# Thirty-two bytes behind the operands: where the rows and buffers that TensorE reads begin in an attention and feed-forward kernel

## The chip, the cores and the metric

The kernel runs on one core of one Trainium2 chip, in one launch. The metric is the time of one execution on the device, in microseconds. Three runs of the kernel before took 712.76, 710.11 and 710.58 us; the median is 710.58 us. One further execution was recorded by the hardware profiler; all rows of the profile come from it.

## The reference

Two attentions in a row, then a feed-forward layer, all in float32. There are 8 batches of 8 heads with 576 tokens and 64 values a head, and 32 learned pack queries a head.

```python
def sm_attn(qq, kk, vv):
    s = scale * np.matmul(qq, kk.transpose(0, 1, 3, 2))
    s = s - np.max(s, axis=-1, keepdims=True)
    a = np.exp(s)
    a = a / (np.sum(a, axis=-1, keepdims=True) + 1e-09)
    return np.matmul(a, vv)
p_packed = sm_attn(p, k, v)                   # 32 packs per head
out = sm_attn(q, p_packed, p_packed)          # each token attends to the packs
...
x = out.transpose(0, 2, 1, 3).reshape(8 * 576, 512)
h = x @ w_in                                  # 512 -> 2048
g = h * (1.0 / (1.0 + np.exp(-h)))
return g @ w_out                              # 2048 -> 512
```

## The kernel before

**Staging.** Per batch, the first attention turns k, v and the pack queries into 32 packed rows a head, and the second gives each token its 32 shares of these rows (a softmax). The product of shares and packed rows isn't formed by itself: the packed rows are first multiplied by w_in (`Packs`, line 461 is the end of it), which gives a matrix from the 256 shares of a token to the 2048 hidden values, and the shares are multiplied by that. So the hidden layer is `h_products` (lines 479 to 489), and the second layer is `products` and `out_products` (lines 516 to 543).

**Halves.** The large products take operands in the type float32r, each number split into an upper part, rounded to that type, and a lower part, the difference. A product is three matmuls: upper by upper, upper by lower, lower by upper. That holds for w_out (`wo_hi`, `wo_lo`, written once, lines 200 and 204), for the shares (`a2_hi`, `a2_lo`, written in `upper2` and `lower2`), for the packs times w_in (`pw_hi`, `pw_lo`, lines 458 and 461) and for the hidden values (`g_hi`, `g_lo`, lines 508 and 514). ScalarE writes the upper parts, VectorE the lower ones.

**Units.** The hidden layer is cut into 16 rows f of 128 values. A unit is one batch and one f: `h_products` makes 12 matmuls of 128x288 columns (two halves of the 576 tokens, two shares of heads, three parts), with a slice of a pack buffer as the stationary operand and a share buffer as the moving one. `h_values` then makes the sigmoid-weighted g of 512 tokens; the 64 tokens left are kept in `rest`, and two batches' rest is done together in four further units. `out_products` makes 12 matmuls of 128x512 columns, with 128 columns of `g_hi` or `g_lo` stationary and a row f of `wo_hi` or `wo_lo` moving. It runs two units behind `h_products`. There are 1536 matmuls of line 489 and 1728 of line 521 in the program.

**Order.** The order of the engines' instructions is written by hand: a list of steps (`ORDER`) for the first two batches, in which w_in and w_out are also decoded from 64-bit loads and split, and the loop over `units` at the end for the other six, in which one step of the next batch's attention is put between units. TensorE, VectorE, ScalarE and SyncE run in that order.

**Buffers.** A pool gives out its buffers in turn. The pack and g pools have two buffers a name, and after the first two batches a third is added in the space that the staging of the weights left (`pw_b`, `gp_b`), so three are in use. The shares have four a name: two halves of the tokens for each of two batches. `wo_hi` and `wo_lo` are one tile each, 16 rows of 512 numbers. Buffers lie one behind the other in the order of the pools.

Of the kernel before, what the change touches and what calls it, by code (L numbers as in the profile page):

```python
# [9 lines left out]
F32 = mybir.dt.float32  # L10
F32R = mybir.dt.float32r
# [4 lines left out]
ALU = mybir.AluOpType  # L16
# [3 lines left out]
P = 128  # L20
# [3 lines left out]
HS = S // 2  # L24
NB = HS // 32
DM = H * D
DFF = 2048
NF = DFF // P
NJ = 4
JW = DFF // NJ  # L30
# [52 lines left out]
def packed_attention_ffn(ctx: ExitStack, tc: tile.TileContext, pkT, qT, vA, vB, w_in, w_out, out):  # L83
# [13 lines left out]
    nc = tc.nc  # L97
    ent = ctx.enter_context
    const = ent(tc.tile_pool(name="const", bufs=1))
    kvq = ent(tc.tile_pool(name="kvq", bufs=2))  # L100
    pw = ent(tc.tile_pool(name="pw", bufs=2))
    a2p = ent(tc.tile_pool(name="a2p", bufs=4))
# [7 lines left out]
    ident = const.tile([P, P], F32, name="ident")  # L110
    make_identity(nc, ident)
    win = const.tile([P, NF, NI, P], I32, name="win")
    wo_hi = const.tile([P, NF, DM], F32R, name="wo_hi")
    wo_lo = const.tile([P, NF, DM], F32R, name="wo_lo")

    rest = const.tile([P, NF, 2, 2, REST], F32, name="rest")
    parts = tc.dram_tile((EARLY, 2, P, 2, DM), F32, name="parts")
# [1 line left out]
    made = {}  # L119
# [34 lines left out]
    class Weights:  # L154
# [38 lines left out]

        def both(self, n):
            f, nf, _ = CHUNKS[n]
            return (t[:, f : f + nf].rearrange("p i n -> p (i n)") for t in (wo_hi, wo_lo))

        def upper(self, n):
            hi, _ = self.both(n)
            nc.scalar.copy(hi, self.raw[n][1].bitcast(F32))  # L200

        def lower(self, n):
            hi, lo = self.both(n)
            nc.vector.tensor_tensor(lo, self.raw[n][1].bitcast(F32), hi.bitcast(F32), ALU.subtract)  # L204

    def heads(bank, lhs, rhs):

# [8 lines left out]
    class Attention:  # L216
# [205 lines left out]
            nc.vector.transpose(s2, e2)  # L422

        def upper2(self, hf):
            hi = a2p.tile([P, 2, HS], F32R, name="a2_hi")
            lo = a2p.tile([P, 2, HS], F32R, name="a2_lo")
            made["a2", self.b, hf] = hi, lo
            a2 = self.back[hf][:, :, :HS] if self.b in ON_TOKENS else self.half[hf][0].rearrange("p (r s) -> p r s", r=2)
            self.shares[hf] = a2
            nc.scalar.copy(hi, a2)  # L430
# [5 lines left out]
    class Packs:  # L436
# [13 lines left out]
        def upper(self):  # L450
            b, j = self.b, self.f // FJ
            if self.f % FJ == 0:
                n = NJ * (b - EARLY) + j
                pool = pw_b if n > 0 and n % 3 == 1 else pw
                made["pw", b, j] = [pool.tile([P, 2, JW], F32R, name=name) for name in ("pw_hi", "pw_lo")]
            c = slice(self.f % FJ * P, (self.f % FJ + self.nf) * P)
            self.hi, self.lo = (t[:, :, c] for t in made["pw", b, j])
            nc.scalar.copy(self.hi, self.ps[:, :, : self.nf * P])  # L458
# [32 lines left out]
    def h_values(u, hf=None):  # L491
        b, f, *more = units[u]
        if hf is None or hf == 0:
            pool = gp_b if u > n_early and (u - n_early) % 3 == 1 else gp
            g_hi = pool.tile([P, 512], F32R, name="g_hi")
            g_lo = pool.tile([P, 512], F32R, name="g_lo")
            if more:
                g = rest[:, f : f + FJ].rearrange("p f e h s -> p (f e h s)")
                nc.scalar.copy(g_hi, g)
                hidden[u] = g, g_hi, g_lo  # L500
                return
            hidden[u] = gp.tile([P, 512], F32, name="g", bufs=1), g_hi, g_lo
        g, g_hi = (x.rearrange("p (h s) -> p h s", h=2) for x in hidden[u][:2])
        ps, to = made.pop(("h", u, hf)), rest[:, f, b % 2]
        if hf is not None:
            ps, to, g, g_hi = ps[:, 0], to[:, hf], g[:, hf], g_hi[:, hf]
        nc.scalar.activation(g, ps[..., :MAIN], AF.Silu)  # L507
        nc.scalar.activation(g_hi, ps[..., :MAIN], AF.Silu)  # L508
        nc.scalar.activation(to, ps[..., MAIN:HS], AF.Silu)  # L509
# [64 lines left out]
    def load_parts(b):  # L574
# [21 lines left out]
        "wl": weights.lower,  # L596
        "h": h_products,
        "g": h_values,
        "l": h_lower,
        "o": out_products,  # L600
# [21 lines left out]
    def hidden_up_to(u):  # L622
        nonlocal done
        while done < min(u, len(units) - 1):
            done += 1
            if len(units[done]) == 2:
                h_products(done)
            h_values(done)
            h_lower(done)
# [116 lines left out]
```

## Time and profile before

| | us |
|---|---|
| median of three runs | 710.58 |
| lowest and highest run | 710.11, 712.76 |
| span of the profiled execution | 711.0 |
| TensorE busy (matmul) | 692.0 |
| VectorE busy | 336.7 |
| ScalarE busy | 326.7 |
| GpSimd busy | 18.0 |

The span is from the first to the last instruction of the profiled execution; no other time is listed for it, and it lies 0.4 us above the median of the runs. Busy times are the union of an engine's instructions. In a row of a group, the first number behind the bar is the union of the busy time of the group, the second the mean duration of one in ns; matmuls overlap, so that a duration is longer than the distance between two starts. Behind the second bar stands how long the engine was idle just before instructions of the group, and what ended that. The operands are named by the program's tiles, output before the arrow.

### The profile page before, as it was taken

How to read it: one execution, taken by the hardware profiler on the slowest of the kernel's cores; microseconds unless marked ns; L12 is line 12 of the kernel's file. 1: busy time of each engine (PE TensorE's matmuls, PEld its weight loads, DVE VectorE, ACT ScalarE, POOL GpSimd, SP SyncE). 2: the span in 40 equal slices, each digit the busy share in tenths (PEclk: the TensorE clock that was granted, in tenths of full speed). 3: DMA queues.
4: the chain of work that ended last, by engine and by line, in shares of the span. 5: the costliest groups of instructions: out<-in, count | busy, mean ns of one | idle time of the engine just before them, and what ended most of it. 6: DMA issues, size and time to landing. Idle time of an engine off the chain costs nothing.

```text
span 711.0 us, 12198 instructions
## 1 busy us (share of the span) xinstructions
PE 692.0 (97%) x5098; PEld 567.0 (80%) x5098; DVE 336.7 (47%) x506; ACT 326.7 (46%) x614; POOL 18.0 (3%) x16
## 2 busy tenths in 40 slices
PE   6789999999999999999999999999999999999997
PEld 4567787878878888888878888878878788888886
DVE  4899997665353336331552315533362333622112
ACT  4577887554434426362532625453352532533221
POOL 0011111110000000000000000000000000000000
PEclk9999999999999999999999999999999999999999
DMA  9858255705012130312111121021301210010002
GB/s 327 322 168 349 76 185 183 265 1 185 1 60 82 33 139 1 111 33 87 67 60 61 39 88 67 27 100 36 137 1 59 83 35 1 1 60 1 0 1 74
DMA packets 31509, 64.15 MB, mean 90 GB/s; under 512 B 19424, under 2 KB 19424, under 8 KB 27104
## 3 DMA queue, kind: packets, MB, share of 16 engines
q1 hardware_dynamic: 31360, 63.26, 25.5%
q8 instruction: 40, 0.66, 0.4%
q10 hardware_dynamic: 96, 0.13, 0.1%
q14 instruction: 13, 0.11, 0.0%
HBM read 47.71 MB, written 11.53 MB: 83 GB/s over the span
## 4 chain that ended last, share of the span: by engine, by line
PE 89%; DVE 6%; DMA 2%; issue 1%; ACT 1%; SPq 0%; DVEq 0%; ACTq 0%
PE ps_acc L521 54%; PE ps_two L489 27%; PE ps_two L211 6%; DMA kvq_t<-in_qT 2%; PE ps_two L309 1%; DVE g_lo L514 1%; DMA kvq_t<-in_pkT 1%; DVE wo_lo L204 1%; DVE win L185 1%; DVE win L191 1%; DVE win L184 0%; DVE win L192 0%; PE ps_acc L211 0%; DVE pw_lo L461 0%; DVE w_raw L184 0%
## 5 line engine op out<-in xcount | busy, mean ns | idle before, releaser
L521 PE MATMUL ps_acc<-wo_hi,g_hi 128*128 128x512 f32 x576 | 229.2, 398 | 0.0
L521 PE MATMUL ps_acc<-wo_lo,g_hi 128*128 128x512 f32 x576 | 225.4, 391 | 0.8 <-DVE wo_lo L204 0.8
L521 PE MATMUL ps_acc<-wo_hi,g_lo 128*128 128x512 f32 x576 | 225.3, 391 | 0.0
L514 DVE TENSOR_TENSOR g_lo<-g,g_hi 128x512 fp32r<-128x512 f32 (+1 forms) x132 | 90.8, 688 | 261.3 <-ACT g_hi L508 261.3
L507 ACT ACTIVATE g<-ps_two 128x512 f32<-128x512 f32 (+1 forms) x132 | 77.5, 587 | 271.2 <-PE ps_two L489 245.6
L489 PE MATMUL ps_two<-a_hi,pw_hi 128*128 128x288 f32 x512 | 152.3, 298 | 2.6 <-DVE pw_lo L461 1.7
L489 PE MATMUL ps_two<-a_lo,pw_hi 128*128 128x288 f32 x512 | 151.5, 296 | 0.0
L489 PE MATMUL ps_two<-a_hi,pw_lo 128*128 128x288 f32 x512 | 150.6, 294 | 0.0
L521 PEld LDWEIGHTS ps_acc<-wo_hi,g_hi 128*128 128x128 f32 x576 | 108.0, 188 | 40.2 <-issue 19.1
L521 PEld LDWEIGHTS ps_acc<-wo_hi,g_lo 128*128 128x128 f32 x576 | 108.1, 188 | 24.4 <-DVE g_lo L514 0.8
L521 PEld LDWEIGHTS ps_acc<-wo_lo,g_hi 128*128 128x128 f32 x576 | 108.2, 188 | 19.6 <-DVE wo_lo L204 1.5
L489 PEld LDWEIGHTS ps_two<-a_hi,pw_hi 128*128 128x128 f32 x512 | 96.4, 188 | 8.1 <-DVE pw_lo L461 2.0
L489 PEld LDWEIGHTS ps_two<-a_lo,pw_hi 128*128 128x128 f32 x512 | 96.1, 188 | 3.5
L489 PEld LDWEIGHTS ps_two<-a_hi,pw_lo 128*128 128x128 f32 x512 | 96.2, 188 | 0.0
L508 ACT ACTIVATE g_hi<-ps_two 128x512 fp32r<-128x512 f32 (+1 forms) x132 | 76.7, 581 | 7.3 <-PE ps_acc L521 7.3
L461 DVE TENSOR_TENSOR pw_lo<-ps_two,pw_hi 128x1024 fp32r<-128x1024 f32 (+1 forms) x35 | 38.3, 1126 | 15.0 <-ACT pw_hi L458 15.0
L458 ACT CAST pw_hi<-ps_two 128x1024 fp32r<-128x1024 f32 (+1 forms) x35 | 31.6, 943 | 21.9 <-PE ps_two L211 21.9
L211 PE MATMUL ps_two<-win,ppT 64*32 64x512 f32 (+1 forms) x560 | 32.5, 560 | 0.4 <-DVE ppT L332 0.4
L509 ACT ACTIVATE rest<-ps_two 128x64 f32<-128x64 f32 (+1 forms) x132 | 30.5, 231 | 0.0
L507 ACT ACT_TABLE_LOAD x15 | 19.2, 1283 | 0.7 <-DVE g_lo L514 0.6
L211 PEld LDWEIGHTS ps_two<-win,ppT 64*32 64x32 f32 x560 | 8.0, 105 | 14.2 <-issue 10.9
L179 ACT ACTIVATE w_raw<-w_raw 128x1024 int32<-128x1024 uint32 (+1 forms) x13 | 13.3, 1021 | 9.5 <-DMA w_raw<-in_w_in 6.2
(101 smaller groups left out, 445.5 us busy)
## 6 DMA issues: line engine op xcount, KB each, us to landing
kvq_t<-in_pkT SPq DMA_DIRECT2D x7, 1216.0 KB, 5.4
kvq_t<-in_vA SPq DMA_DIRECT2D x8, 1024.0 KB, 6.9
out<-o SPq DMA_DIRECT2D x16, 512.0 KB, 2.9
kvq_t<-in_qT SPq DMA_DIRECT2D x7, 1152.0 KB, 5.1
w_raw<-in_w_in SPq DMA_DIRECT2D x6, 1024.0 KB, 8.4
win<-in_w_out SPq DMA_DIRECT2D x3, 1024.0 KB, 6.5
w_raw<-in_w_out SPq DMA_DIRECT2D x3, 1024.0 KB, 4.9
tm<-tm SPq DMA_DIRECT2D x56, 40.0 KB, 2.0
```

Of the source, the lines that this page charges most:

```text
L179: nc.scalar.activation(low, low.bitcast(U32), AF.Copy, scale=2.0**-29)
L185: nc.vector.scalar_tensor_tensor(low, up, -(2**31), low, op0=ALU.bitwise_and, op1=ALU.bitwise_or)
L191: nc.vector.tensor_scalar(z, up, 3, None, op0=ALU.logical_shift_left)
L211: nc.tensor.matmul(bank(par)[NP * i : NP * i + NP], lhs(r, i), rhs(r, i), start=True, stop=True)
L458: nc.scalar.copy(self.hi, self.ps[:, :, : self.nf * P])
L461: nc.vector.tensor_tensor(self.lo, self.ps[:, :, : self.nf * P], self.hi.bitcast(F32), ALU.subtract)
L489: nc.tensor.matmul(bank, p[:, par, cols], a[:, par], start=(n == 0), stop=(n == len(todo) - 1))
L507: nc.scalar.activation(g, ps[..., :MAIN], AF.Silu)
L508: nc.scalar.activation(g_hi, ps[..., :MAIN], AF.Silu)
L509: nc.scalar.activation(to, ps[..., MAIN:HS], AF.Silu)
L514: nc.vector.tensor_tensor(g_lo[:, c], g[:, c], g_hi[:, c].bitcast(F32), ALU.subtract)
L521: nc.tensor.matmul(bank, g[:, rows], w[:, f], start=(first and n == 0), stop=(last and n == 2))
```

## The change

w_out's halves get rows of 520 numbers, of which 512 are used. Each buffer of the shares, of g's halves and of the packs gets 8 numbers more at its end, which nothing reads or writes. The copies that split w_out take their source and target as rows instead of one flat run, since the target is no longer one. The rest of the program, its order, the number of instructions and the numbers that are computed stay as they are. `both` (line 194 and on) gives the two halves' rows of a chunk of one or two.

```diff
@@ -110,8 +110,8 @@
     ident = const.tile([P, P], F32, name="ident")
     make_identity(nc, ident)
     win = const.tile([P, NF, NI, P], I32, name="win")
-    wo_hi = const.tile([P, NF, DM], F32R, name="wo_hi")
-    wo_lo = const.tile([P, NF, DM], F32R, name="wo_lo")
+    wo_hi = const.tile([P, NF, DM + 8], F32R, name="wo_hi")[:, :, :DM]
+    wo_lo = const.tile([P, NF, DM + 8], F32R, name="wo_lo")[:, :, :DM]
 
     rest = const.tile([P, NF, 2, 2, REST], F32, name="rest")
     parts = tc.dram_tile((EARLY, 2, P, 2, DM), F32, name="parts")
@@ -193,15 +193,15 @@
 
         def both(self, n):
             f, nf, _ = CHUNKS[n]
-            return (t[:, f : f + nf].rearrange("p i n -> p (i n)") for t in (wo_hi, wo_lo))
+            return (t[:, f : f + nf] for t in (wo_hi, wo_lo))
 
         def upper(self, n):
             hi, _ = self.both(n)
-            nc.scalar.copy(hi, self.raw[n][1].bitcast(F32))
+            nc.scalar.copy(hi, self.raw[n][1].bitcast(F32).rearrange("p (f n) -> p f n", n=DM))
 
         def lower(self, n):
             hi, lo = self.both(n)
-            nc.vector.tensor_tensor(lo, self.raw[n][1].bitcast(F32), hi.bitcast(F32), ALU.subtract)
+            nc.vector.tensor_tensor(lo, self.raw[n][1].bitcast(F32).rearrange("p (f n) -> p f n", n=DM), hi.bitcast(F32), ALU.subtract)
 
     def heads(bank, lhs, rhs):
 
@@ -422,8 +422,8 @@
             nc.vector.transpose(s2, e2)
 
         def upper2(self, hf):
-            hi = a2p.tile([P, 2, HS], F32R, name="a2_hi")
-            lo = a2p.tile([P, 2, HS], F32R, name="a2_lo")
+            hi = a2p.tile([P, 2 * HS + 8], F32R, name="a2_hi")[:, : 2 * HS].rearrange("p (r s) -> p r s", r=2)
+            lo = a2p.tile([P, 2 * HS + 8], F32R, name="a2_lo")[:, : 2 * HS].rearrange("p (r s) -> p r s", r=2)
             made["a2", self.b, hf] = hi, lo
             a2 = self.back[hf][:, :, :HS] if self.b in ON_TOKENS else self.half[hf][0].rearrange("p (r s) -> p r s", r=2)
             self.shares[hf] = a2
@@ -452,7 +452,10 @@
             if self.f % FJ == 0:
                 n = NJ * (b - EARLY) + j
                 pool = pw_b if n > 0 and n % 3 == 1 else pw
-                made["pw", b, j] = [pool.tile([P, 2, JW], F32R, name=name) for name in ("pw_hi", "pw_lo")]
+                made["pw", b, j] = [
+                    pool.tile([P, 2 * JW + 8], F32R, name=name)[:, : 2 * JW].rearrange("p (r s) -> p r s", r=2)
+                    for name in ("pw_hi", "pw_lo")
+                ]
             c = slice(self.f % FJ * P, (self.f % FJ + self.nf) * P)
             self.hi, self.lo = (t[:, :, c] for t in made["pw", b, j])
             nc.scalar.copy(self.hi, self.ps[:, :, : self.nf * P])
@@ -492,8 +495,8 @@
         b, f, *more = units[u]
         if hf is None or hf == 0:
             pool = gp_b if u > n_early and (u - n_early) % 3 == 1 else gp
-            g_hi = pool.tile([P, 512], F32R, name="g_hi")
-            g_lo = pool.tile([P, 512], F32R, name="g_lo")
+            g_hi = pool.tile([P, 512 + 8], F32R, name="g_hi")[:, :512]
+            g_lo = pool.tile([P, 512 + 8], F32R, name="g_lo")[:, :512]
             if more:
                 g = rest[:, f : f + FJ].rearrange("p f e h s -> p (f e h s)")
                 nc.scalar.copy(g_hi, g)
```

A number has four bytes, so a row of w_out's halves takes 2080 bytes in place of 2048, a share buffer 2336 in place of 2304, a g half 2080 in place of 2048, and a pack buffer 4128 in place of 4096.

## The prediction

> **What bounds the kernel now.** I read the page first (share of each engine, the chain that ended last, the costliest groups), then the chain in order of time, then the timeline of TensorE in a quiet stretch.
>
> ```profile
> PE 692.0 (97%) x5098; PEld 567.0 (80%) x5098; DVE 336.7 (47%) x506; ACT 326.7 (46%) x614; POOL 18.0 (3%) x16
> PE 89%; DVE 6%; DMA 2%; issue 1%; ACT 1%; SPq 0%; DVEq 0%; ACTq 0%
> L521 PE MATMUL ps_acc<-wo_hi,g_hi 128*128 128x512 f32 x576 | 229.2, 398 | 0.0
> L521 PE MATMUL ps_acc<-wo_lo,g_hi 128*128 128x512 f32 x576 | 225.4, 391 | 0.8 <-DVE wo_lo L204 0.8
> L521 PE MATMUL ps_acc<-wo_hi,g_lo 128*128 128x512 f32 x576 | 225.3, 391 | 0.0
> L489 PE MATMUL ps_two<-a_hi,pw_hi 128*128 128x288 f32 x512 | 152.3, 298 | 2.6 <-DVE pw_lo L461 1.7
> L489 PE MATMUL ps_two<-a_lo,pw_hi 128*128 128x288 f32 x512 | 151.5, 296 | 0.0
> L489 PE MATMUL ps_two<-a_hi,pw_lo 128*128 128x288 f32 x512 | 150.6, 294 | 0.0
> ```
>
> TensorE holds 89% of the chain, and before these two lines it was idle for 3.4 us in all. So the kernel ends when TensorE has got through its list: 3 x 576 = 1728 matmuls of 512 columns (line 521) and 3 x 512 = 1536 of 288 columns (line 489). Both operands of every one of these 3264 lie in the buffers that the change pads. The means of 391 to 398 and 294 to 298 ns aren't what one costs, since matmuls overlap: what counts is how far apart they start. That stands in the timeline (start, duration, engine, line, operands):
>
> ```profile
> 373.20 0.29 PE L489 MATMUL ps_two<-a_hi,pw_hi 128*128 128x288 f32 x1
> ...
> 374.67 0.29 PE L489 MATMUL ps_two<-a_hi,pw_lo 128*128 128x288 f32 x1
> ...
> 375.94 0.39 PE L521 MATMUL ps_acc<-wo_hi,g_lo 128*128 128x512 f32 x1
> ...
> 377.30 0.39 PE L521 MATMUL ps_acc<-wo_hi,g_lo 128*128 128x512 f32 x1
> 377.53 0.29 PE L489 MATMUL ps_two<-a_hi,pw_hi 128*128 128x288 f32 x1
> 377.66 0.29 PE L489 MATMUL ps_two<-a_lo,pw_hi 128*128 128x288 f32 x1
> 377.79 0.29 PE L489 MATMUL ps_two<-a_hi,pw_lo 128*128 128x288 f32 x1
> 377.92 0.30 PE L489 MATMUL ps_two<-a_hi,pw_hi 128*128 128x288 f32 x1
> 378.06 0.29 PE L489 MATMUL ps_two<-a_lo,pw_hi 128*128 128x288 f32 x1
> ...
> 378.99 0.29 PE L489 MATMUL ps_two<-a_hi,pw_lo 128*128 128x288 f32 x1
> ...
> 380.27 0.39 PE L521 MATMUL ps_acc<-wo_hi,g_lo 128*128 128x512 f32 x1
> ...
> 381.63 0.39 PE L521 MATMUL ps_acc<-wo_hi,g_lo 128*128 128x512 f32 x1
> ```
>
> Between 375.94 and 377.30 lie six starts of line 521: 1.36 / 6 = 226.7 ns each. The unit after it, with another g buffer and another row of w_out, has 1.36 / 6 again. Line 489 starts 12 matmuls from 373.20 to 374.67 and 12 from 377.53 to 378.99: (1.47 + 1.46) / 22 = 133.2 ns each. The two lines differ by 224 columns and 93.5 ns, 0.417 ns a column. So 512 columns stream in 213.7 ns and 288 in 120.2, and **some 13 ns of each matmul don't depend on its length**. Over all of them this fixed part is 3264 x 13 = 42.4 us, 6.0% of the span. If the places of the operands cost TensorE anything now, it sits in there: the rest is columns.
>
> **Where the operands begin now.** By the shapes, every tile up to the g buffers that these matmuls read is a multiple of 128 bytes long: w_out's halves 32768 bytes with rows of 2048, a share buffer 2304, a pack buffer 4096, a g buffer 2048. So whatever the buffer, row or slice, all operands begin at the same place within 128 bytes. Whether larger differences of place matter, the chain in order of time can tell (start, length, what):
>
> ```profile
> 223.84 3.19 PE ps_two L489 x24
> 227.03 2.77 PE ps_acc L521 x12
> 241.30 2.77 PE ps_acc L521 x12
> 362.41 10.95 PE ps_acc L521 x48
> 572.92 3.19 PE ps_two L489 x24
> 591.10 2.77 PE ps_acc L521 x12
> ```
>
> From 227 to 591 us the units go through 16 rows of w_out, three g buffers, three pairs of pack buffers and all share buffers, in ever new pairs, and the lengths of like pieces repeat to the hundredth of a microsecond: 2.77 for 12 of line 521, 3.19 for 24 of line 489. Steps of 128 bytes and more therefore change nothing. What the trace can't show is a step below 128 bytes, and that is just what the change brings.
>
> **The change part by part.**
>
> *w_out's halves.* A row grows from 2048 to 2080 bytes, so row f begins 32 f bytes further on: at 0, 32, 64 and 96 within 128 bytes in turn. Three of four moving streams of line 521 begin elsewhere than now. No matmul is added or gets longer. The direct cost at TensorE is nothing or unknown, bounded below.
>
> *Splitting w_out (lines 200 and 204).* The copies and subtractions now write rows with a gap. No instruction is added. A 1024-element one covers two rows, and the dearest reading is that it costs as much as two of one row:
>
> ```profile
> L200 ACT CAST wo_hi<-win x5: 674/1130/1178, 46.2 to 104.4; 128x1024 fp32r<-128x1024 f32 x3, 128x512 fp32r<-128x512 f32 x2
> L200 ACT CAST wo_hi<-w_raw x5: 653/1133/1153, 17.0 to 149.8; 128x1024 fp32r<-128x1024 f32 x3, 128x512 fp32r<-128x512 f32 x2
> L204 DVE TENSOR_TENSOR wo_lo<-w_raw,wo_hi x5: 679/1216/1225, 18.2 to 152.6; 128x1024 fp32r<-128x1024 f32 x3, 128x512 fp32r<-128x512 f32 x2
> ```
>
> The two-row forms from w_raw take 1133 and 1216 ns, twice the one-row form would be 1306 and 1358: at most 173 + 142 = 315 ns for each of six pairs (three that come from w_raw and three from win), 1.9 us if all of it were on the path. A gap between rows is no new instruction, and the idle rows show TensorE waiting 0.8 us for line 204 in all, so I take nothing and keep 1.9 us as the end. Below nothing I see no reason.
>
> *Shares, g and packs.* Successive buffers step by 32 bytes. Of four share buffers, two g_hi and two g_lo, two pw_hi and two pw_lo, each kind is spread over the places within 128 bytes; the slices inside one buffer stay 512 or 1152 bytes apart, so they keep its place. ScalarE and VectorE do the same work on them. Should that become dearer, it is covered:
>
> ```profile
> L514 DVE TENSOR_TENSOR g_lo<-g,g_hi 128x512 fp32r<-128x512 f32 (+1 forms) x132 | 90.8, 688 | 261.3 <-ACT g_hi L508 261.3
> L507 ACT ACTIVATE g<-ps_two 128x512 f32<-128x512 f32 (+1 forms) x132 | 77.5, 587 | 271.2 <-PE ps_two L489 245.6
> ```
>
> VectorE stands idle 261.3 us ahead of g_lo and ScalarE 271.2 us ahead of g, and no row above has TensorE waiting for g. If a tenth came on top of both (9.1 and 7.8 us), this cover would swallow it.
>
> *TensorE's streams, the one term that decides.* Cost from both sides. The gain can't exceed the fixed part, 42.4 us. A loss is sized by the same rows: 13 ns are some 31 columns at 0.417 ns, and 31 columns of four bytes are about 128 bytes. If a stream paid for each 128-byte piece that it touches, one that starts inside a piece would touch one more, and pay 13 ns. I take zero, because it is nearest to the row that there is (no difference over all larger steps), and keep both ends.
>
> The Trainium skill, "TensorE: Matmul & The Clock Gate" (Step-by-step: what each phase is for), speaks against a gain: weights and moving data have independent read ports, so that loading the next weights takes nothing from the running matmul; by it the term is zero. The same page (Back-to-back issue gap) gives N/2.4 + 2.5 ns between warm matmuls, 215.8 ns for 512 columns; the trace has 226.7, so there are some 10.9 ns that this rule doesn't explain, as an estimate 18.8 us over the 1728 matmuls of this kind. "SBUF — State Buffer" (Door 1: The DMA port swizzle) counts in lines of 16 bytes; padding of 32 bytes would then make no stream touch one line more, which speaks against the loss. No run here shows lines or ports as such.
>
> *Sum.* 711.0 us of span, plus 0 for the streams, plus 0 for the rest: 711.0 us. The median of the runs shown is 710.58, the profiled span 0.4 us above it, so the time forecast is **710.6 us**. Within 0.5% (3.6 us, about what a measurement of this kernel can tell from no change) counts as the same.
>
> **The rivals.**
>
> *Faster: the fixed part is a meeting of two reads.* The next weights load while a matmul streams, and both now begin at the same place within 128 bytes. If they get in each other's way for that reason, pairs with different places would be free of it. For it: a fixed part of 13 ns exists whose cause no row names, and this start-up isn't even the same each time, as the first rows of line 489 show, 130 ns apart (377.53 to 377.92) and then 140. Against it: it was unmoved by every pairing of buffers. Price: if one of four relative places is free, 3264 / 4 x 13 = 10.6 us, 700.0 us; if three of four are, 31.8 us, 678.8 us.
>
> *Slower: a start inside a piece costs one piece more.* The place is each stream's first read, the price is worked out above, and it decides from the first matmul on whose moving row begins off the grid. With pieces of 128 bytes three of four starts are off it: 0.75 x 3264 x 13 = 31.8 us, 742.4 us. With pieces of 64 bytes only the places 32 and 96 are, half of all, for half the time: 0.5 x 3264 x 6.5 = 10.6 us, 721.2 us. For it: the fixed part is just one such piece long, in both kinds. Against it: a matmul that starts on the grid already pays it, which looks more like a change of weights than like a piece read.
>
> *It doesn't do what it says.* If only the relative place counted, equal places would stay in about a quarter of the pairs, which is in the prices above; no other way is open.
>
> **How the numbers follow.** No effect, 707.0 to 714.1 us: 0.52. Faster by some 10.6 us: 0.17; by 31.8: 0.09. Slower by some 10.6 us: 0.14; by 31.8: 0.08. That is faster 0.26, same 0.52, slower 0.22. The two far cases, 0.17 together, stay out of the range; the two near ones set its ends, 700.0 and 721.2 us; the 1.9 us of the splitting lies within it. The likeliest case alone has 707.0 to 714.1.
>
> **What would show it.** If I'm right, six starts of line 521 still span 1.36 us in a quiet stretch, the like pieces of the chain still read 2.77 and 3.19 us, and line 204 stays near 1216 ns. In the faster case the starts come 214 to 224 ns apart, differently from unit to unit, as the places meet; in the slower case by 233 or 240 ns in one half or three quarters of the rows of w_out, the same rows in each batch, while rows 0, 4, 8 and 12 keep 226.7. A change of more than 1.9 us ahead of 150 us, with unchanged starts, would mean that the splitting is what I mis-sized. The forecast fails if TensorE reads by places finer than 128 bytes, of which the trace before holds no sample.

## The result and the profile after

| | before | after |
|---|---|---|
| median of four runs, us | 711.16 (710.11 to 712.76) | 717.00 (715.88 to 718.97) |
| span of the profiled execution, us | 711.0 | 717.2 |
| ratio after to before | | 1.0084, 95% interval 1.0059 to 1.0108 |

The change makes the kernel 0.8% slower, 5.8 us between the medians. The profiled execution of after took 718.97 us for its span of 717.2: 1.8 us lie around the span, which the prediction had not set apart. A ratio is reckoned over the runs of both kernels and isn't quite the quotient of the medians. One execution of a later kernel, that with a space of 128 bytes, took 973.16 us at a granted clock of 0.657; it is left out of that kernel's ratio, and its profile isn't used.

The page of after, in the parts that answer to those shown of before (lines 489 and 521 are now 492 and 524):

```profile
PE 698.4 (97%) x5098; PEld 567.9 (79%) x5098; DVE 337.0 (47%) x506; ACT 326.5 (46%) x614; POOL 17.9 (3%) x16
PE 90%; DVE 5%; DMA 2%; ACT 1%; issue 1%; SPq 0%; DVEq 0%; ACTq 0%
L524 PE MATMUL ps_acc<-wo_hi,g_hi 128*128 128x512 f32 x576 | 231.5, 402 | 0.0
L524 PE MATMUL ps_acc<-wo_lo,g_hi 128*128 128x512 f32 x576 | 227.1, 394 | 0.6 <-DVE wo_lo L204 0.6
L524 PE MATMUL ps_acc<-wo_hi,g_lo 128*128 128x512 f32 x576 | 227.2, 394 | 0.0
L492 PE MATMUL ps_two<-a_hi,pw_hi 128*128 128x288 f32 x512 | 152.3, 298 | 2.3 <-ACT rest L512 1.5
L492 PE MATMUL ps_two<-a_lo,pw_hi 128*128 128x288 f32 x512 | 151.4, 296 | 0.0
L492 PE MATMUL ps_two<-a_hi,pw_lo 128*128 128x288 f32 x512 | 151.3, 295 | 0.0
```

TensorE's share of the chain went from 89% to 90%, and it waits no more than before. VectorE and ScalarE did the same work in the same time. Only the matmuls of 512 columns differ: means of 402, 394 and 394 ns where 398, 391 and 391 stood. The busy time of these three rows grew from 229.2 + 225.4 + 225.3 = 679.9 to 231.5 + 227.1 + 227.2 = 685.8 us, by 5.9 us, which is the whole loss. Those of 288 columns read as before within 1 ns, 298, 296 and 295. The timeline of a quiet unit shows it as a distance between starts:

```profile
379.20 0.40 PE L524 MATMUL ps_acc<-wo_hi,g_lo 128*128 128x512 f32 x1
...
380.61 0.40 PE L524 MATMUL ps_acc<-wo_hi,g_lo 128*128 128x512 f32 x1
```

Six starts take 1.41 us, 235 ns each, where 226.7 stood in both quiet units of before; whole units of after, of 12 starts, average 229 to 234 ns where nothing stops them. The chain in order of time has two undisturbed runs of 48 such matmuls, which make a good gauge; a run of 12 stands ahead of them:

```profile
229.23 2.78 PE ps_acc L524 x12
...
365.49 11.14 PE ps_acc L524 x48
...
534.17 11.14 PE ps_acc L524 x48
```

Before, the first of them took 10.95 us and the second 10.92:

```profile
529.84 10.92 PE ps_acc L521 x48
```

The difference of 0.19 to 0.22 us is 4.0 to 4.6 ns a matmul. Times 1728 that is 6.8 to 7.9 us, more than the whole loss, since short runs can lose less: the one shown takes 2.78 us where 2.77 stood. The split copies, the other candidate, kept their duration (median 1220 ns where 1216 stood):

```profile
L204 DVE TENSOR_TENSOR wo_lo<-w_raw,wo_hi x5: 685/1220/1226, 18.3 to 154.1; 128x1024 fp32r<-128x1024 f32 x3, 128x512 fp32r<-128x512 f32 x2
```

### The profile page after: what moved, and what is told of

Same layout as the page of the kernel before. It is cut to its first block, busy times and chain, and to the rows that moved or that the text cites. A ratio compares the mean times of both kernels' runs of the same rounds, so it can differ in the third digit from the quotient of the medians.

```text
span 717.2 us, 12198 instructions
## 1 busy us (share of the span) xinstructions
PE 698.4 (97%) x5098; PEld 567.9 (79%) x5098; DVE 337.0 (47%) x506; ACT 326.5 (46%) x614; POOL 17.9 (3%) x16
## 4 chain that ended last, share of the span: by engine, by line
PE 90%; DVE 5%; DMA 2%; ACT 1%; issue 1%; SPq 0%; DVEq 0%; ACTq 0%
PE ps_acc L524 55%; PE ps_two L492 27%; PE ps_two L211 6%; DMA kvq_t<-in_qT 2%; PE ps_two L309 1%; DVE g_lo L517 1%; DMA kvq_t<-in_pkT 1%; PE ps_two L132 1%; DVE win L191 0%; DVE wo_lo L204 0%; DVE win L185 0%; DVE win L184 0%; PE ps_acc L211 0%; DVE w_raw L184 0%; DVE win L192 0%
## 5 line engine op out<-in xcount | busy, mean ns | idle before, releaser
L524 PE MATMUL ps_acc<-wo_hi,g_hi 128*128 128x512 f32 x576 | 231.5, 402 | 0.0
L524 PE MATMUL ps_acc<-wo_lo,g_hi 128*128 128x512 f32 x576 | 227.1, 394 | 0.6 <-DVE wo_lo L204 0.6
L524 PE MATMUL ps_acc<-wo_hi,g_lo 128*128 128x512 f32 x576 | 227.2, 394 | 0.0
```

The lines of the kernel that those rows point to most:

```text
L524: nc.tensor.matmul(bank, g[:, rows], w[:, f], start=(first and n == 0), stop=(last and n == 2))
```

## The experiments

**Theories.** A: a stream of matmuls runs at its best while all stationary operands begin at one place within 128 bytes, and loses it where they alternate. B: a moving operand that begins off the 128-byte grid pays. C: the distance from the stationary operand's start to the moving one's counts. Each part of the change was tried alone, and the streams by themselves.

### Streams by themselves

The computation is left out. After a warm-up, 36 matmuls in a row run for each pair of places m (moving) and w (stationary), in bytes.

```diff
+    for n, ms, ws in cases():
...
+            for k in range(COUNT):
+                m = ms[k % len(ms)] // 4 + 512 * (k // 12 % 3)
+                w = ws[k % len(ws)] // 4 + 128 * (k % 12)
+                nc.tensor.matmul(ps[:, :n], wts[:, w : w + P], mov[:, m : m + n], start=(k == 0), stop=(k == COUNT - 1))
```

> Leaves out the whole computation; 36 matmuls in a row for each pair of patterns: n columns, byte places m of the moving operand and w of the stationary one, repeated in turn. Theory A (a stream settles at 226.7 ns a start for 512 columns and 133.3 for 288 when all stationary operands begin at one place, and can't settle while they alternate): every case with one m and one w takes 36 x 226.7 = 8.2 us (288: 4.8 us) besides its last matmul's tail, whatever m and w; w = 0,0,x and w = 0,x take 231 ns or more a start, 8.3 to 8.5 us. Theory B (a moving stream that begins off the 128-byte grid pays): the cases with m = 16 to 112 and w = 0 are longer, w = 16 to 96 with m = 0 are not, m = 32 with w = 32 is longer too. Theory C (the distance between the moving and the stationary place counts): m = x, w = 0 and m = 0, w = x differ from m = w = 0, and m = w = 32 does not.

The timeline, each case one row (start and length in us). In the order shown: m = w = 0; m = 4, 16 and 32 with w = 0; m = 0 with w = 32 and 96; m = 0 with w = 0, 0, 16 in turn; w = 0, 0, 32; m = w = 32; and, with 288 columns, m = 4 with w = 0.

```profile
27.90 8.45 PE L135 MATMUL n_m_w__147<-mov,wts 128*128 128x512 f32 x36
36.41 8.80 PE L135 MATMUL n_m_w__188<-mov,wts 128*128 128x512 f32 x36
...
54.01 8.60 PE L135 MATMUL n_m_w__270<-mov,wts 128*128 128x512 f32 x36
62.67 8.67 PE L135 MATMUL n_m_w__311<-mov,wts 128*128 128x512 f32 x36
...
124.05 8.66 PE L135 MATMUL n_m_w__599<-mov,wts 128*128 128x512 f32 x36
...
141.50 8.70 PE L135 MATMUL n_m_w__681<-mov,wts 128*128 128x512 f32 x36
150.26 8.43 PE L135 MATMUL n_m_w__722<-mov,wts 128*128 128x512 f32 x36
158.74 8.67 PE L135 MATMUL n_m_w__763<-mov,wts 128*128 128x512 f32 x36
...
307.19 8.46 PE L135 MATMUL n_m_w__1462<-mov,wts 128*128 128x512 f32 x36
...
321.44 5.15 PE L135 MATMUL n_m_w__1545<-mov,wts 128*128 128x288 f32 x36
```

A falls: with one place for each operand throughout, m = 32 still takes 8.67 us and w = 32 8.66, 0.22 / 35 = 6.3 ns a start more than 8.45. B falls: w = 32 costs as much with the moving operand on the grid, and m = w = 32, both off the grid, is as short as m = w = 0 within 0.01 us. C holds in these pairs: with 512 columns the distance counts and not either place by itself, and of the fixed distances tried zero is best. A changing distance costs too (w = 0, 0, 32), with one exception among those tried, w = 0, 0, 16.

### One part of the change at a time

Each kernel keeps one edit of the diff and drops the others.

```diff
 # w_out's rows alone
+    wo_hi = const.tile([P, NF, DM + 8], F32R, name="wo_hi")[:, :, :DM]
+    wo_lo = const.tile([P, NF, DM + 8], F32R, name="wo_lo")[:, :, :DM]
 # g alone
+            g_hi = pool.tile([P, 512 + 8], F32R, name="g_hi")[:, :512]
+            g_lo = pool.tile([P, 512 + 8], F32R, name="g_lo")[:, :512]
 # shares and packs alone
+            hi = a2p.tile([P, 2 * HS + 8], F32R, name="a2_hi")[:, : 2 * HS].rearrange("p (r s) -> p r s", r=2)
...
+                    pool.tile([P, 2 * JW + 8], F32R, name=name)[:, : 2 * JW].rearrange("p (r s) -> p r s", r=2)
```

> w_out's rows alone keep their 32 bytes. Theory A: in a unit all matmuls still have one moving place and one stationary place, so line 521's starts settle at 226.7 ns as before and the time is 711 us. Theory B: three of four rows begin off the grid and carry nearly all of the loss, 716 to 717 us. Theory C: three of four units have a distance that isn't zero, 714 to 717 us.

> g's halves alone keep their 32 bytes, so g_hi and g_lo of a unit begin at different places while all rows of w_out begin on the grid. Theory A: all of the loss is here, 716 to 717 us, with units of 12 at 2.98 us in place of 2.77 and 2.94. Theory B: 711 us. Theory C: a loss here as well, 714 to 717 us.

> The shares and the packs alone keep their 32 bytes; only line 489's operands move. All theories: line 521 is untouched and settles as before; line 489, whose mean start distance fell from 133.0 to 132.6 ns over some 1420 of them with the whole change, gains 0.6 us or nothing, 710 to 711 us. If the loss came from line 489's effect on what follows it, 714 us or more.

| kept | median, us | before on the same chip | ratio, 95% interval |
|---|---|---|---|
| w_out's rows | 718.46 | 711.97 | 1.0085, 1.0068 to 1.0103 |
| g's halves | 717.22 | 711.97 | 1.0069, 1.0053 to 1.0085 |
| shares and packs | 716.59 | 711.97 | 1.0067, 1.0047 to 1.0087 |

Each part alone brings about the whole loss, so the parts don't add up. In the trace of w_out's rows alone the distance can be read row by row, since row f begins 32 f bytes further on. These are the runs of 12 of rows 2, 5, 8 and 10 of one batch, at 64, 160, 256 and 320 bytes:

```profile
227.93 2.76 PE ps_acc L524 x12
...
242.28 2.81 PE ps_acc L524 x12
...
257.44 2.73 PE ps_acc L524 x12
...
267.49 2.76 PE ps_acc L524 x12
```

Row 8, at 256 bytes, reads 2.73 us, the least that the chain of before shows; row 5 is the slowest, and rows 2 and 10, 256 bytes apart, are alike. Row 0, at distance 0, reads 2.77 and not 2.73: its starts settle only towards the end of the run, behind a row 15 that lies off.

The third part is the surprise, against what all theories said: it pads nothing that the 512-column matmuls read. Yet these are the ones that lose, in the chain of that kernel:

```profile
365.82 11.09 PE ps_acc L524 x48
...
534.41 11.09 PE ps_acc L524 x48
```

The explanation lies in the order of the buffers. Shares and packs stand between w_out's halves and g. Their padding, 8 x 32 + 4 x 32 = 384 bytes, moves two of the three g buffers against w_out by 384 bytes, and the third, behind two more pack buffers, by 448. By the sizes of the tiles, with each small one counted up to a multiple of 32 bytes, all from w_out to g add up to a whole number of 512 bytes in the kernel before, so that the distance was 0 within 512 for every matmul of line 521. That is worked out from the program; no view shows an address, and the runs that follow test it. It gives theory D: line 521 runs at its best only while this distance is 0, within 512 bytes or some part of it.

### Moving g by 128 bytes, and back

The first kernel is that of before with one unused space ahead of g; no operand is padded, but all that lies behind the space moves too, the third pack buffers among it. The second has the padded shares and packs, and two spaces that bring g back to its distance.

```diff
 # first kernel, on the kernel before
+    ent(tc.tile_pool(name="space", bufs=1)).tile([P, 32], F32, name="space")
     gp = ent(tc.tile_pool(name="gp", bufs=2))
 # second kernel, on shares and packs alone
+    ent(tc.tile_pool(name="space", bufs=1)).tile([P, 32], F32, name="space")
     gp = ent(tc.tile_pool(name="gp", bufs=2))
...
+    ent(tc.tile_pool(name="space_b", bufs=1)).tile([P, 112], F32, name="space_b")
     gp_b = ent(tc.tile_pool(name="gp_b", bufs=1))
```

> The kernel before with one unused space of 128 bytes ahead of the g buffers: nothing else is padded, and every operand still begins on the 128-byte grid, but g now lies 128 bytes off w_out's rows within 512 bytes, where it lay 0 off. Theory D (line 521 settles at 226.7 ns only while the distance from the stationary to the moving place is a multiple of 512 bytes): all of line 521 is thrown off, 716 to 717 us, units of 12 at 2.97 to 3.00 us. Rival E (only places within 128 bytes count): 711 us, units at 2.77 and 2.94 us.

> As with the shares and packs alone padded, and two unused spaces more, of 128 and 448 bytes, that put all g buffers back to a distance of 0 from w_out's rows within 512 bytes. Theory D: line 521 settles again, 710 to 712 us, and what is left of the loss of the shares and packs is line 489's own, under 1 us. Rival (line 489's new places throw off what follows): 716 us as without the spaces.

The space alone costs as much as the whole change: 718.7 us against 712.55, ratio 1.0096 (1.0077 to 1.0115). Put back, the padded shares and packs cost nothing: 711.42 us, ratio 0.9991 (0.9976 to 1.0006), and the runs of 48 (line 525 in this kernel) are at 10.93 and 10.95 us:

```profile
361.68 10.93 PE ps_acc L525 x48
...
529.12 10.95 PE ps_acc L525 x48
```

### Which distances

Again streams by themselves, now over the range of 512 bytes, with the stationary operands as in the kernel (three matmuls on each slice, two buffers).

```diff
+    out = [(288, (16 * i,) * 12, 0) for i in range(32)]
+    out += [(288, (16 * i,) * 3 + (16 * i + 128,) * 3, 0) for i in range(0, 32, 2)]
+    out += [(512, (m,) * 12, 0) for m in (0, 128, 192, 256, 320, 384, 448)]
+    out += [(512, (0,) * 12, w) for w in (128, 256, 384)]
```

> Leaves out the whole computation; 36 matmuls in a row a case, the stationary operand as in the kernel (three matmuls on a slice, two buffers), the moving one at a given distance. Theory D: of 512 columns at 0, 128, 192, 256, 320, 384, 448 bytes only 0 takes 226.7 ns a start, the others 229 to 235, and moving the stationary operand by 128, 256, 384 costs the same as moving the other one by 384, 256, 128. For 288 columns, where 48 bytes took 130.0 ns and 0 took 131.7, places of 130 ns or less are to be found among the 32. Rival E: 128, 256 and 384 read as 0.

Timeline of the cases: of 288 columns at distances 0, 16, 32, then 112 and then 272; of 512 columns with the moving operand at 0, 128, 192, 256, and then with the stationary one at 128, 256, 384.

```profile
30.24 5.01 PE L124 MATMUL case_aa<-mov,wts 128*128 128x288 f32 x36 [0.68 <-ACT o L116]
35.31 4.95 PE L124 MATMUL case_ab<-mov,wts 128*128 128x288 f32 x36
40.31 5.06 PE L124 MATMUL case_ac<-mov,wts 128*128 128x288 f32 x36
...
65.68 5.10 PE L124 MATMUL case_ah<-mov,wts 128*128 128x288 f32 x36
...
116.71 4.95 PE L124 MATMUL case_ar<-mov,wts 128*128 128x288 f32 x36
...
274.80 8.43 PE L124 MATMUL case_bw<-mov,wts 128*128 128x512 f32 x36
283.28 8.63 PE L124 MATMUL case_bx<-mov,wts 128*128 128x512 f32 x36
291.97 8.66 PE L124 MATMUL case_by<-mov,wts 128*128 128x512 f32 x36
300.68 8.45 PE L124 MATMUL case_bz<-mov,wts 128*128 128x512 f32 x36
...
335.20 8.64 PE L124 MATMUL case_cd<-mov,wts 128*128 128x512 f32 x36
343.90 8.46 PE L124 MATMUL case_ce<-mov,wts 128*128 128x512 f32 x36
352.42 8.64 PE L124 MATMUL case_cf<-mov,wts 128*128 128x512 f32 x36
```

Distance 256 is as good as 0, whichever operand is moved (8.45 and 8.46 us), 128 and 384 cost 0.2 us in 36. The period is 256 bytes, half of what was supposed. For 288 columns 16 bytes is better than 0, 32 is worse and 112 worst, and 272 repeats 16, as each of the 16 steps from 256 on repeats the one 256 bytes ahead of it within 0.01 us. In the kernel this can be asked with a space of 256 bytes where 128 had cost 6 us:

```diff
+    ent(tc.tile_pool(name="space", bufs=1)).tile([P, 64], F32, name="space")
     gp = ent(tc.tile_pool(name="gp", bufs=2))
```

> The kernel before with one unused space of 256 bytes ahead of the g buffers, where 128 bytes cost 6 us. If the distance counts within 256 bytes, as the map of distances says, line 521 settles as before and the time is 711 to 712.5 us. If it counts within 512 bytes, 716 to 718 us.

It took 711.54 us against 712.06, ratio 0.9993 (0.9979 to 1.0006): 256 bytes are free. All that lies behind the space moved here too, so the loss with 128 bytes comes from the distance and not from moving things as such.

### Better places for the other line

Before, line 489 was not at its best. A model of the kernel's units, 12 matmuls of 288 and 12 of 512 columns in turn, was run with many sets of places; all computation but TensorE's order is left out.

```diff
+    for x in (16, 32, 48, 64, 80, 96, 112):
+        add(p0=x, p1=x)
+    for x in (16, 32, 48, 64, 96):
+        add(a1=x)
...
+    for x in (16, 32, 64):
+        add(g1=x)
...
+    add(g0=128, g1=128)
```

> Leaves out the whole computation but the order of TensorE: four units of 12 matmuls of 288 and 12 of 512 columns a case, with the places of before in the first case, and in each further case one set of places moved. Theory D: the first case takes 4 x 4.33 us = 17.3 us; moving g alone by 64 or 128 bytes makes it some 0.2 us longer; moving the packs against the shares changes only the part of 288 columns, by up to 4 x 12 x 3 ns = 0.15 us either way.

Moving g by 128 bytes (case_bg) lengthens the 512-column part of a case (48 matmuls, first number behind the bar) from the 11.6 us of before's places (case_aa) to 11.8, as expected. Against the expectation, moving the lower shares alone by 16 bytes (case_ai) lengthens the same part, whose own places it leaves alone:

```profile
L149 PE MATMUL case_bg<-mov,wts 128*128 128x512 f32 x48 | 11.8, 395 | 0.0
...
L149 PE MATMUL case_ai<-mov,wts 128*128 128x512 f32 x48 | 11.8, 393 | 0.0
...
L149 PE MATMUL case_aa<-mov,wts 128*128 128x512 f32 x48 | 11.6, 390 | 0.0
```

So what runs ahead of line 521 counts as well. A second model took 185 sets for shares and packs, three units each; the loops shown make 144 of them.

```diff
+    for a1 in (0, 32, 96):
+        for p1 in range(0, 256, 32):
+            for p0 in (0, 32, 64, 96, 112, 128):
+                add(a1=a1, p0=p0, p1=p1)
...
```

> Leaves out the whole computation but the order of TensorE, as with the units before, three units a case: w_out and g stay at a distance of 0, and the packs' upper and lower parts and the shares' lower part take 184 sets of places. If only line 489's own settling counts, the best sets lie 12 x 3 = 36 ns a unit under the first one; if line 521's start suffers from what ran ahead of it, the sets with the shortest part of 288 columns are not the ones with the shortest unit.

The timeline of three sets; two starts of the 288-column part are one unit apart. First the places of before, then the lower packs on by 32 bytes, then the upper packs on by 112 and the lower packs and lower shares by 32.

```profile
35.21 1.76 PE L136 MATMUL case_aa<-mov,wts 128*128 128x288 f32 x12
...
39.54 1.76 PE L136 MATMUL case_aa<-mov,wts 128*128 128x288 f32 x12
...
128.63 1.74 PE L136 MATMUL case_ah<-mov,wts 128*128 128x288 f32 x12
...
132.94 1.74 PE L136 MATMUL case_ah<-mov,wts 128*128 128x288 f32 x12
...
821.52 1.74 PE L136 MATMUL case_ch<-mov,wts 128*128 128x288 f32 x12
...
825.82 1.74 PE L136 MATMUL case_ch<-mov,wts 128*128 128x288 f32 x12
```

Units of 4.33, 4.31 and 4.30 us, the last the shortest of all sets. The set with the shortest part of 288 columns isn't the one with the shortest unit: its unit takes 4.32 us. The last two sets shown went into the kernel, with 256 bytes of room so that all else keeps its distance:

```diff
 # lower packs 32 bytes on
+                    pool.tile([P, 2 * JW + pad], F32R, name=name)[:, pad // 8 : pad // 8 + 2 * JW].rearrange("p (r s) -> p r s", r=2)
+                    for name, pad in (("pw_hi", 0), ("pw_lo", 64))
 # best set
+                    pool.tile([P, 2 * JW + 64], F32R, name=name)[:, at : at + 2 * JW].rearrange("p (r s) -> p r s", r=2)
+                    for name, at in (("pw_hi", 28), ("pw_lo", 8))
...
+            lo = a2p.tile([P, 2 * HS + 64], F32R, name="a2_lo")[:, 8 : 8 + 2 * HS].rearrange("p (r s) -> p r s", r=2)
```

> The kernel before with the lower halves of the packs alone moved on by 32 bytes within 256, all other distances kept (the third g buffers move by 256). The units alone gained 20 ns each so (4307 ns in place of 4327): 128 x 20 ns = 2.6 us, 709 us. If the stretches with two parts of line 489 in a row or with other work between behave otherwise, 711 us as before. A loss of 4 us or more would mean that 256 bytes do count for line 521 in the kernel.

> The kernel before with the places of the best of the 185 cases of units: the packs' upper halves 112 bytes on, their lower halves 32, the shares' lower halves 32, all else at its distance of before within 256 bytes. Units of 4300 ns in place of 4327: 128 x 27 ns = 3.5 us, 707 to 708.5 us. If the units of a model don't carry over, it isn't better than with the lower packs alone moved, 708.8 us.

| places | median, us | before on the same chip | ratio, 95% interval |
|---|---|---|---|
| lower packs 32 bytes on | 708.81 | 711.73 | 0.9949, 0.9929 to 0.9968 |
| best set of the model | 707.88 | 712.06 | 0.9944, 0.9923 to 0.9966 |

Both beat both kernels; between the two the intervals don't decide. In the chain of the first, 24 matmuls of 288 columns take 3.15 us where 3.19 stood, and 12 of 512 columns behind them 2.73 where 2.77 stood:

```profile
223.12 3.15 PE ps_two L492 x24
226.27 2.73 PE ps_acc L524 x12
```

## Why the prediction was right and wrong

**What bounds the kernel and the gauge were right.** TensorE's list sets the end, the splitting of w_out cost nothing (1220 ns against 1216), ScalarE and VectorE stayed covered, and the one term that could move was the streams' distance between starts. The measured 717.0 us lies in the range, between the forecast of no effect and the near slower case of 721.2. That the range reaches so far is owed to that rival, whose cause was wrong, and so the hit is partly luck.

**The likeliest case was wrong.** 5.8 us is more than the 0.5% that counted as the same. The step that failed is "Steps of 128 bytes and more therefore change nothing." The trace of before could not carry it: in all its pairs of line 521 the two operands lay a multiple of 512 bytes apart, so the many buffers and rows were one sample, repeated. Nor were the like pieces alike by themselves. The prediction took those that stand behind 24 matmuls of line 489; elsewhere in the same chain runs of 12 of line 521 read 2.73 and 2.94 us, by what ran ahead of them:

```profile
220.90 2.94 PE ps_acc L521 x12
...
231.40 2.73 PE ps_acc L521 x12
```

The first spacer of 128 bytes refuted the step, at 718.7 us. The prediction checked that each operand stayed on the grid, and not by how much the pairs differed.

**The sizes.** Zero was taken for the streams. What was measured is 4.0 to 4.6 ns for each of 48 in a row, where the bound was the fixed 13 ns, so the loss lies within the bound. The 13 ns themselves aren't firm. They come from line 489 at 133.2 ns, and the streams show that this figure goes by the places: with 130.0 ns, which 288 columns took at 48 bytes, the same working gives (226.7 - 130.0) / 224 = 0.432 ns a column and leaves about 6 ns. The change in line 489's own streams is too small to see in the means (298, 296, 295 ns against 298, 296, 294).

**The rivals.** The faster one named the right quantity, the relative place of the two operands, and had the wrong sign: equal places are the good case for 512 columns, and the kernel before had them everywhere. The slower one had the right sign and the wrong cause. It said that rows 0, 4, 8 and 12 would keep 226.7 ns, and that a start off the grid pays; but both operands 32 bytes off the grid run at their best, and with every operand on the grid one spacer of 128 bytes costs it all. That the parts don't add up follows from the cause: a pair at distance zero can be spoilt only once.

The rule weighed in the prediction, that loading weights takes nothing from a running matmul (the Trainium skill, "TensorE: Matmul & The Clock Gate", Step-by-step: what each phase is for), gave zero for the term. The term isn't zero: with nothing but the distance of the two operands changed, from 0 to 192 bytes, 36 matmuls take 8.43 or 8.66 us. Whether it is the two reads that meet, or something else that goes by both addresses, no run here shows; that stays open. That it is the distance, and not g's own place, rests on the streams with m = w = 32: no kernel moved both operands of line 521 alike.

## What to carry to other kernels

Where TensorE sets the pace, the distance between the start of the stationary and of the moving operand is a property of the layout worth keeping: compare pairs of operands, not each one with a grid, and look at what any new or padded tile does to all that lie behind it. A value that never varies in a trace isn't shown to be without effect. Places are best chosen with a model of the instruction order that runs many sets at once, and then tried in the kernel, since they are worth 0.5% one way and 0.7 to 1.0% the other here.

## What the runs showed of the hardware

A stream of like float32r matmuls, each with its own stationary operand, settles into a repeating pattern of starts: 226, 227 and 227 ns apart with 512 columns at distance 0, and 228 to 241 ns at 128 bytes. The mean of the pattern depends on the distance between the two operands' starts within 256 bytes: with 512 columns 36 matmuls take from 8.43 to 8.46 us at 0 or 256 bytes to 8.80 at 4 bytes, and with 288 columns from 4.95 us at 16 or 272 to 5.15 at 4. The best distance isn't the same for both lengths. Even at the best distance tried, 512 columns keep 226.7 ns a start; how much of it doesn't depend on the length, 6 or 13 ns or something else, no run here settles.
